# Gate and up of the feed-forward block: S1 T1 by a second Strassen level in four pairs, in one written order for three engines

## The chip, the cores and the metric

The kernel runs on one core of one Trainium2 chip. The metric is the device time of one execution in microseconds (us). All matrix products are done on TensorE (PE in the profile); VectorE (DVE) does the additions and subtractions, ScalarE (ACT) copies, the high parts and the GELU; SyncE (SP) and GpSimd (POOL) issue transfers between SBUF and DRAM.

## The reference, cut to what matters

```
x = A_x                                    # 1 x 2048 x 640
g = sigmoid((x * gate_w).sum(-1))
a = Re(DFT_seq(DFT_hidden(x)))             # DFT matrices given, as products
b = (gelu(x @ w_gate) * (x @ w_up)) @ w_down   # 640 -> 1728 -> 640
out = g * a + (1 - g) * b
```

All inputs are float32. The stage that the change touches is the pair of products `x @ w_gate` and `x @ w_up`.

## The kernel before, in words

Each float32 operand is split into a high part, rounded to the fp32r format of TensorE, and a low part, the rest. A product is then three matmuls of 128x128 by 128x512 (`mm3`): high times high, high times low, low times high. `split` makes the parts: the high one on ScalarE (`high`), the low one on VectorE (`low`), which needs the high one.

The 1728 hidden columns are 13 blocks of 128 and a rest of 64. Block 0 and the rest are computed first, plainly. Blocks f = 1 to 12 use Strassen's scheme with seven products on a two-by-two matrix whose rows of blocks are gate and up and whose columns are halves of the 640 inputs (the fifth 128 rows are extra products, `g5`, `u5` and `D`). The tokens are handled as two halves tp of two 512-token tiles each. The weights' sums are called S1 to S4, the tokens' sums T1 to T4; the results collect in PSUM banks X and Z.

Blocks 1 and 2 run through `gate_up`. From block 3 on, two blocks make a pair p (p = 1 to 5): `pair_first` computes the gate's and the up's first products of both blocks and both token halves by a second Strassen level (J = 1 and 2: sums of weights from `pair_parts`, sums of tokens from `cross_sums`, which go to the DRAM tiles `xtd` and come back by `load_cross`). Then `chain` runs for each of the two blocks and both token halves the other products: S1 T1, S2 T2, S3 T3, S4 with its extra product, and A22 T4. In the old kernel S1 T1 of a pair takes eight mm3 (two blocks, two token halves, two input halves), and a pair 70 mm3.

What sets the order: TensorE, VectorE and ScalarE each work through their instructions in the order of the built program. A scheduler of the language makes that order from the dependencies, except inside `in_order(...)`, where each named engine keeps the order in which the code was written. In the old pairs only TensorE has a written order, and only in `pair_first`. `seed` copies a PSUM bank into a new bank on ScalarE, so that two sums can go on from one partial sum. `chain_parts(f)` makes the four weight sums S1 to S4 of a block (four VectorE operations of 256 elements and one of 128), and splits them: 1024 elements on each of the two engines. `extras` puts other work into the pairs: weight sums for later stages (`sum_wd`, `sum_wu`, stored to DRAM) and the gate's row sums (`load_z`, a VectorE reduction). All loads are issued in order on SP's queue, most into a ring of 48 buffers (`slot`), where a new tile waits until the last use of its buffer is over; results are stored from POOL's queue (`keep`).

After the pairs comes the down stage (`load_k`, `split_k`, `step_k`), then the sequence DFT (the C stage: `load_c`, `split_c`), then the hidden DFT. From the down stage on, ScalarE and VectorE have a written order.

Of the kernel before, what the change touches and what calls it, by code (L numbers as in the profile page):

```python
# [23 lines left out]
NK = (NF - 1) // 2  # L24
XN_AT = [5, 10, 15, 20]
EORD = [0, 2, 1, 3, 4]


@with_exitstack
def kernel(  # L30
# [84 lines left out]
    uA, uT = ([[dram.tile([P, 4, T], F32, tag=f"u{n}{j}{p}", name=f"u{n}{j}{p}") for p in range(ND)] for j in range(2)] for n in "AT")  # L115
    xtd = {J: dram.tile([P, 3, 2, T], F32, tag=f"xtd{J}", name=f"xtd{J}") for J in (1, 2)}
    grd, gmd = (dram.tile([1, S], F32, tag=n, name=n) for n in ("grd", "gmd"))
# [22 lines left out]
    def load_x(tp):  # L140
# [23 lines left out]
        def tsum(i):  # L164

            a, b = {1: ((1, 2), (1, 1)), 2: ((2, 2), "T1"), 3: ((2, 2), (1, 2)), 4: ((2, 1), "T2")}[i]
            r[f"T{i}"] = pair(F32, f"xs{n}{i}")
            tt(r[f"T{i}"], r[a], r[b], op=ALU.subtract)
            B[f"T{i}"] = hl(f"xT{n}{i}")

        def his(*keys):
# [59 lines left out]

    def chain_parts(f, raw, W):

        ra, rb = raw
        sm, *c = wchunk(f"ws{f}")
        g01, g23, u23 = ra[:, 0:2], ra[:, 2:4], ra[:, 5:7]
        tt(sm[:, 0:2], rb, u23, op=ALU.add)
        tt(sm[:, 4:6], g01, rb, op=ALU.subtract)
        tt(sm[:, 2:4], sm[:, 0:2], g01, op=ALU.subtract)
        tt(sm[:, 6:8], g23, sm[:, 2:4], op=ALU.subtract)  # L240
        d = wsmall(F32R, f"wd{f}")
        split(*c, sm)
        tt(rb[:, 1], ra[:, 4], ra[:, 7], op=ALU.subtract)
        split(d[:, 0], d[:, 1], rb[:, 1])
        W["D"] = d[:, 0], d[:, 1]
        for i in range(2):
            for k in range(4):
                W[f"S{k + 1}", i] = at(c, 2 * k + i)

# [8 lines left out]
    def pair_parts(p, r0, r1):  # L258
# [16 lines left out]
        return W  # L275

    def cross_loads(J):

        r = [pair(F32, f"xc{J}{q}") for q in range(2)]
        for q in range(2):  # L280
            nc.sync.dma_start(r[q], xt[2 * q, 2 * J - 2 : 2 * J].rearrange("d p c -> p d c"))
        return r
# [138 lines left out]
    def pair_first(p, WP, W):  # L421
# [59 lines left out]
        return X, s1  # L481

    def chain(f, W, B, tp, s5, X, s1):

# [22 lines left out]
        tt(s2, s2, Z, op=ALU.add)  # L507
        last_products(X, W, B, tp, k, second, s1, s2, s5, prod)
        yield

    def last_products(X, W, B, tp, k, second, s1, s2, s5, prod):

# [3 lines left out]
        if second:  # L516
# [4 lines left out]
            keep(hT[tp][k], 1, t1)  # L521
        prod(X, "A22", "T4", False)
        mm3(X, W["u5"], at(B[5], 0), False, True)
        tt(s1, s1, X, op=ALU.mult)
        keep(hA[tp][k], 2 * second, s1)
        if second:
            tt(s5, s1, t1, op=ALU.subtract)
# [16 lines left out]
    def sum_wd(k):  # L544

        r, a21 = slot(F32, [P, 8, P], f"dr{k}"), wsmall(F32, f"da{k}")
        nc.sync.dma_start(r, wd[k, :, :8])
        nc.sync.dma_start(a21, wd[k, :, 8:])
        sums_left(f"d{k}", r, a21, wsd[k])

    def sum_wu(p):


        r, a21 = slot(F32, [P, 8, P], f"ur{p}"), wsmall(F32, f"ua{p}")
        nc.sync.dma_start(r, wu[p, :, :8])
        nc.sync.dma_start(a21, wu[p, :, 8:])
        if p > 1:
            v, r = r, slot(F32, [P, 8, P], f"un{p}")
            for a, b in ((0, 2), (2, 4), (4, 5), (5, 8)):
                kept = p == 4 and a in (0, 4)  # L560
                nc.scalar.activation(r[:, a:b], v[:, a:b], AF.Copy, scale=1.0 if kept else -1.0)
            if p < 4:
                v, a21 = a21, wsmall(F32, f"ub{p}")
                nc.scalar.activation(a21, v, AF.Copy, scale=-1.0)
            nc.gpsimd.dma_start(wneg[p], r)
        sums_left(f"u{p}", r, a21, wsu[p])

# [17 lines left out]
    def load_z(sb):  # L585

        r = slot(F32, [P, D], f"xz{sb}")
        nc.sync.dma_start(r, xz[sb])
        nc.vector.tensor_tensor_reduce(r, r, gwb, 1.0, 0.0, ALU.mult, ALU.add, z[:, sb : sb + 1])

# [312 lines left out]
    sq = [lambda k=k: sum_wd(k) for k in range(NK)]  # L903
    for p in range(ND):
        sq.insert(2 * p + 1, lambda p=p: sum_wu(p))

    def extras():
        sq.pop(0)()
        for _ in range(2):
            if zq:  # L910
                load_z(zq.pop(0))

# [25 lines left out]
    for i in (1, 2):  # L938
        for J in (2, 1):
            load_cross(J, i)  # L940
    chain_parts(3, raws[0], Ws[0])
    for p in range(1, NK):
        f = 2 * p + 1
        for J in (2, 1):
            load_cross(J, 4)
        with in_order(PE):
            X, s1 = pair_first(p, WP, Ws)
        for i in range(2):
            s5 = pair(F32, f"s5{f + i}")
            work = [chain(f + i, Ws[i], Bs[tp], tp, s5[:, tp], X[i, tp], s1[i, tp]) for tp in range(2)]  # L950
            for step in range(4):
                for w in work:
                    next(w)
                if (i, step) == (0, 0):
                    chain_parts(f + 1, raws[1], Ws[1])
                if i == 0 and step in (1, 3):
                    extras()
                if p == NK - 1:
                    if (i, step) == (0, 0):
                        gate_rows()  # L960
                    if (i, step) == (0, 2):
                        extras()
                    if (i, step) == (0, 3):
                        load_k(0)
                    if (i, step) == (1, 0):
                        split_k(0)
                    if i == 1 and step >= 1:
                        load_k(step)
                    continue
                if (i, step) == (0, 2):  # L970
                    nraws = load_raw(f + 2), load_raw(f + 3)
                if (i, step) == (1, 0):
                    raws = nraws
                    WP = pair_parts(p + 1, raws[0][0], raws[1][0])
                if (i, step) == (1, 1):
                    nWs = [plain_parts(f + 2 + i, raws[i][0]) for i in range(2)]
                    for J in (2, 1):
                        load_cross(J, 1)
                if (i, step) == (1, 2):
                    chain_parts(f + 2, raws[0], nWs[0])  # L980
                    load_cross(2, 2)
                if (i, step) == (1, 3):
                    load_cross(1, 2)
                    Ws = nWs
    order = ctx.enter_context(ExitStack())
# [360 lines left out]
```

## Time and profile before

| | us |
|---|---|
| median of three runs (lowest to highest) | 1026.31 (1026.24 to 1027.57) |
| the profiled execution | 1026.11 |
| its span | 1024.3 |
| TensorE busy, 4500 matmuls | 1017.2 |
| VectorE busy | 794.1 |
| ScalarE busy | 478.1 |

The span is what the trace covers; the execution's own time is a little longer. TensorE's busy time counts overlapping matmuls once, so an engine shown busy may still have some idle time between its matmuls; the spacing of matmuls in the timeline is the sharper measure. Of the span, the pairs p = 1 to 5 take the stretch from about 96 to 336 us.

### The profile page before, as it was taken

Reading aid. Unit: us, or ns where it says so; the run is one execution under the profiler, and the core shown is the slowest. Engines: PE = TensorE matmul, PEld = TensorE weight load, DVE = VectorE, ACT = ScalarE, POOL = GpSimd, SP = SyncE. Lnnn points to the kernel's source line nnn. Section 1 sums busy time; section 2 is a strip of 40 time slices with the busy share of each in tenths; the row PEclk is TensorE's granted clock in tenths of the full one; section 3 lists DMA queues with packets and bytes.
Section 4 is the critical chain, followed back from the end, with each engine's and each line's share of the span. In section 5 each row is a group of like instructions: output and inputs, shape, how many; then the busy total and the mean of one; then the engine's idle time right before and its main releaser. Section 6 shows DMA issues by size and latency. Waiting matters only on the chain.

```text
span 1024.3 us, 12988 instructions
## 1 busy us (share of the span) xinstructions
PE 1017.2 (99%) x4500; PEld 839.3 (82%) x4500; DVE 794.1 (78%) x1099; ACT 478.1 (47%) x631; POOL 137.4 (13%) x245
## 2 busy tenths in 40 slices
PE   9999999999999999999999999999999999999998
PEld 6888778888888888888888888888888888888887
DVE  6998777777866949976898966786577769697784
ACT  5455443555463647466355443444343354355430
POOL 0023121212122200100010011002000200021013
PEclk9999999999999999999999999999999999999999
DMA  8258767776888987867866677557666777897748
GB/s 300 80 205 278 273 246 269 256 273 240 301 286 328 389 319 251 272 245 267 310 202 232 214 223 263 191 195 243 240 203 209 276 258 287 290 331 219 269 97 131
DMA packets 84914, 255.04 MB, mean 249 GB/s; under 512 B 10768, under 2 KB 18992, under 8 KB 84848
## 3 DMA queue, kind: packets, MB, share of 16 engines
q1 hardware_dynamic: 63376, 187.13, 53.4%
q0 software_dynamic: 21328, 66.88, 19.3%
q8 instruction: 35, 0.57, 0.2%
q14 instruction: 31, 0.25, 0.1%
q10 hardware_dynamic: 144, 0.20, 0.1%
HBM read 187.04 MB, written 67.13 MB: 248 GB/s over the span
## 4 chain that ended last, share of the span: by engine, by line
PE 97%; DMA 2%; DVE 0%; ACT 0%; issue 0%; SPq 0%
PE pZ L87 5%; PE pZ L85 4%; PE pZ L86 4%; PE pX L85 4%; PE pX L87 4%; PE pX L86 4%; PE pL L85 3%; PE pL L86 3%; PE pL L87 3%; PE px L85 3%; PE px L86 3%; PE px L87 3%; PE pV L85 2%; PE pV L86 2%; PE pV L87 2%; DMA xx<-xtd 1%
## 5 line engine op out<-in xcount | busy, mean ns | idle before, releaser
L74 ACT ACTIVATE ch<-csa 128x1024 fp32r<-128x1024 f32 x32 | 34.0, 1062 | 88.4 <-DVE csa L638 53.8
L74 ACT ACTIVATE ch<-cra 128x1024 fp32r<-128x1024 f32 x32 | 33.9, 1058 | 48.5 <-DVE cl L77 18.1
L77 DVE TENSOR_TENSOR cl<-cra,ch 128x1024 fp32r<-128x1024 f32 x32 | 39.1, 1223 | 16.2 <-ACT ch L74 15.9
L77 DVE TENSOR_TENSOR cl<-crb,ch 128x1024 fp32r<-128x1024 f32 x32 | 39.1, 1222 | 15.0 <-ACT ch L74 8.3
L86 PE MATMUL pL<-cl,xah 128*128 128x512 f32 x128 | 49.8, 389 | 0.0
L87 PE MATMUL pL<-ch,xal 128*128 128x512 f32 x128 | 49.8, 389 | 0.0
L85 PE MATMUL pL<-ch,xah 128*128 128x512 f32 x128 | 49.3, 389 | 0.0
L77 DVE TENSOR_TENSOR cl<-csb,ch 128x1024 fp32r<-128x1024 f32 x32 | 39.2, 1224 | 6.2 <-ACT ch L74 4.7
L74 ACT ACTIVATE ch<-crb 128x1024 fp32r<-128x1024 f32 x32 | 33.8, 1055 | 19.5 <-DVE cl L77 7.8
L77 DVE TENSOR_TENSOR cl<-csa,ch 128x1024 fp32r<-128x1024 f32 x32 | 39.1, 1222 | 4.0 <-ACT ch L74 3.3
L307 POOL DMA_DIRECT2D hA<-s x48 | 26.1, 543 | 101.3 <-DVE s L514 39.8
L74 ACT ACTIVATE ch<-csb 128x1024 fp32r<-128x1024 f32 x32 | 33.9, 1059 | 11.9 <-PE pL L86 6.9
L513 ACT ACTIVATE s<-s 128x512 f32<-128x512 f32 x20 | 12.6, 630 | 56.2 <-DVE s L507 56.2
L77 DVE TENSOR_TENSOR kl<-kw,kh 128x1024 fp32r<-128x1024 f32 (+1 forms) x26 | 31.5, 1211 | 6.9 <-ACT kh L74 6.9
L74 ACT ACTIVATE kh<-kw 128x1024 fp32r<-128x1024 f32 (+1 forms) x26 | 27.1, 1041 | 10.8 <-DVE kw L696 3.5
L1052 POOL DMA_DIRECT2D uA<-s x16 | 8.7, 543 | 158.4 <-DVE s L1098 151.8
L307 POOL DMA_DIRECT2D hT<-s x48 | 26.1, 544 | 22.5 <-DMA hT<-s 5.1
L751 POOL DMA_DIRECT2D out<-ks x12 | 6.5, 543 | 167.3 <-DVE ks L750 166.7
L87 PEld LDWEIGHTS pL<-ch,xal 128*128 128x128 f32 x128 | 24.0, 188 | 5.0
L85 PEld LDWEIGHTS pL<-ch,xah 128*128 128x128 f32 x128 | 24.0, 188 | 5.0
L86 PEld LDWEIGHTS pL<-cl,xah 128*128 128x128 f32 x128 | 24.0, 188 | 5.0
L637 DVE TENSOR_TENSOR csa<-cra 128x512 f32<-128x512 f32 x32 | 22.0, 687 | 7.5 <-PE pL L86 6.5
(3041 smaller groups left out, 3407.4 us busy)
## 6 DMA issues: line engine op xcount, KB each, us to landing
cra<-in_ct SPq DMA_DIRECT2D x64, 512.0 KB, 4.0
crb<-in_ct SPq DMA_DIRECT2D x64, 512.0 KB, 4.8
xx<-xtd SPq DMA_DIRECT2D x30, 512.0 KB, 5.5
hA<-s POOLq DMA_DIRECT2D x48, 256.0 KB, 5.8
hT<-s POOLq DMA_DIRECT2D x48, 256.0 KB, 7.3
kr<-hA SPq DMA_DIRECT2D x24, 512.0 KB, 7.1
kr<-hT SPq DMA_DIRECT2D x24, 512.0 KB, 7.1
ux<-uA SPq DMA_DIRECT2D x24, 512.0 KB, 5.2
```

What stands on the lines that cost most here:

```text
L74: nc.scalar.activation(hi, raw, AF.Copy)
L77: nc.vector.tensor_tensor(lo, raw, hi.bitcast(F32), op=ALU.subtract)
L85: nc.tensor.matmul(ps, lh, rh, start=first, stop=False, skip_group_check=True)
L86: nc.tensor.matmul(ps, lh, rl, start=False, stop=False, skip_group_check=True)
L87: nc.tensor.matmul(ps, ll, rh, start=False, stop=last, skip_group_check=True)
L307: nc.gpsimd.dma_start(to[:, i], src)
L513: nc.scalar.activation(s2, s2, AF.Gelu_apprx_tanh)
L637: tt(s1[:, 0], r1[:, 1], r1[:, 0], op=ALU.subtract)
L751: nc.gpsimd.dma_start(out[2 * tp + t, e], src)
L1052: nc.gpsimd.dma_start(to[:, i], src)
```

## The change

Pairs 2 to 5 no longer run `pair_first` and `chain` but one generator, `whole_pair`. Pair 1 stays as it was, and gains the sums for a third token set, J = 3, made of T1 (which is kept in DRAM, `xt1`). In a whole pair S1 T1 of both blocks and both token halves is done by seven mm3 with the second level's sums (`fifth_parts`, banks `Z`), so a pair has 69 mm3. Its `yield` numbers count mm3; what else has to be done is written between them, in `in_order(PE, ACT, DVE)`. Three of the weight sums (`sum_wu` for p = 2 to 4) move from the pairs into the C stage, at its steps 17, 20 and 34, and are computed one step after their loads are issued. `chain_parts`, `sum_wd`, `sum_wu` and `load_z` now return their arithmetic as a function, to be called later. The weights' parts of block f (`chain_parts(f)`), which were made in the pair before, are now made inside the pair.

```diff
+WU_AT = [17, 20, 34]
...
-    def chain_parts(f, raw, W):
+    def chain_parts(f, raw, W, again=False):
...
+        tt(rb[:, 1], ra[:, 4], ra[:, 7], op=ALU.subtract)
         d = wsmall(F32R, f"wd{f}")
-        split(*c, sm)
-        tt(rb[:, 1], ra[:, 4], ra[:, 7], op=ALU.subtract)
-        split(d[:, 0], d[:, 1], rb[:, 1])
...
+        def parts():
+            split(*c, sm)
+            split(d[:, 0], d[:, 1], rb[:, 1])
+            if again:
+                W["raw"] = mtile(F32, f"wr{f}")[:, : 2 * P].rearrange("q (i c) -> q i c", i=2)
+                nc.scalar.activation(W["raw"], sm[:, 0:2], AF.Copy)
...
+    def fifth_parts(p, W0, W1):
+
+        a, b = W0["raw"], W1["raw"]
+        e = mtile(F32, f"fs{p}").rearrange("q (k c) -> q k c", k=4)
+        tt(e[:, 0], b[:, 0], b[:, 1], op=ALU.add)
+        tt(e[:, 2], a[:, 0], b[:, 0], op=ALU.subtract)
+        tt(e[:, 1], e[:, 0], a[:, 0], op=ALU.subtract)
+        tt(e[:, 3], a[:, 1], e[:, 1], op=ALU.subtract)
+        h = slot(F32R, [P, 2, 4, P], f"fh{p}")
+        split(h[:, 0], h[:, 1], e)
...
+    def whole_pair(p, WP, Ws, raws):
...
+        yield 3
+        m(v00, 2, "a12", "b21")
+        m(va, 2, "s2", "t2")
+        v01 = seed(va, f"pv01{p}")
+        m(X[0, 0], 1, "a12", "b21")
+        m(xa_, 1, "s2", "t2")
+        X[0, 1] = seed(xa_, f"px01{p}")
+        sv, sx = copy(ve, f"sv{p}"), copy(xe, f"sx{p}")
+        s1[0, 0] = copy(X[0, 0], f"s100{p}")
+        yield 7
+        fifth(v00, 0, "g5", 0, 0)
+        plus(s1[0, 0], v00)
+        m(v01, 2, "s4", "b22")
+        m(va, 2, "s3", "t3")
+        v10 = seed(va, f"pv10{p}")
+        yield 10
...
+        prod(X[0, 0], 0, "S2", "T2", 0)
+        state(0, 0)
+        plus(s1[1, 1], sv)
+        yield 19
...
+        fifth(Z[0, 1], 0, "u5", 1, 1)
+        plus(Z[0, 1], sz)
+        nc.scalar.activation(s5[0][:, 1], Z[0, 1], AF.Copy)
+        plus(s5[0][:, 1], X[0, 1])
+        m(Z[1, 0], 3, "a22", "t4")
+        yield 38
...
+        with in_order(PE, ACT, DVE):
+            for u in whole_pair(p, WP, Ws, raws):
+                if u == 3:
+                    parts = chain_parts(f, raws[0], Ws[0], True)
+                    for i in (1, 2, 4):
+                        load_cross(3, i)
+                if u == 7:
+                    parts()
+                if u == 13:
+                    parts = chain_parts(f + 1, raws[1], Ws[1])
+                if u == 16:
+                    parts()
+                if u == 19:
+                    WP[3] = fifth_parts(p, *Ws)
+                    todo = extras()
+                if u == 29:
+                    if todo:
+                        todo.pop(0)()
+                    todo += extras()
+                if u == 38:
+                    for do in todo:
+                        do()
+                if more:
+                    if u == 32:
+                        nraws = load_raw(f + 2), load_raw(f + 3)
+                    if u == 47:
+                        nWP = pair_parts(p + 1, nraws[0][0], nraws[1][0])
...
+                else:
+                    if u == 47:
+                        gate_rows()
+                        load_k(0)
...
+                    if u == 59:
+                        split_k(0)
...
+        if i in WU_AT:
+            wu_sums = sum_wu(2 + WU_AT.index(i))
+        if i - 1 in WU_AT:
+            wu_sums()
```

**Place 1, the end of pair 2 on ScalarE in the old program.** `ws7h` is the high part of the sums of block 7, the first of pair 3; `vh3`, `ve3` are parts of the second-level weights of pair 3; `pva3` and `pxa3` are the first banks of pair 3; `pZ6` is bank Z of block 6.

```order
L497 ACTIVATE s56_1628<-pZ6_0_1629 128x512
L497 ACTIVATE s56_1628<-pZ6_1_1640 128x512
L132 ACTIVATE s26_0_1672<-px102_1440 128x512
L74 ACTIVATE vh3_1652<-vs3_1651 128x1024
L132 ACTIVATE s26_1_1680<-pxa2_1377 128x512
L74 ACTIVATE ve3_1654<-wa7_1552 128x512
L74 ACTIVATE wp7_1682<-wa7_1552 128x512
L74 ACTIVATE wp8_1685<-wa8_1556 128x512
L74 ACTIVATE wd7_1713<-wb7_1553 128x128
L74 ACTIVATE ws7h_1707<-ws7r_1706 128x1024
L513 ACTIVATE s26_0_1672<-s26_0_1672 128x512
L513 ACTIVATE s26_1_1680<-s26_1_1680 128x512
```

In the old program the first seed of pair 3 is the row behind these, so `ws7h` stands ahead of all its seeds; and the copies of Z6 stand ahead of `vh3`.

The same `ws7h` on ScalarE in the changed program, inside pair 3. `px013`, `pv103` and `px103` are seeds into new banks, `sv3`, `sx3`, `s1003` and `s1013` copies from banks.

```order
L444 ACTIVATE px013_1873<-pxa3_1825 128x512
L134 ACTIVATE sv3_1875<-pve3_1826 128x512
L134 ACTIVATE sx3_1877<-pxe3_1827 128x512
L134 ACTIVATE s1003_1879<-px003_1836 128x512
L75 ACTIVATE ws7h_1845<-ws7r_1844 128x1024
L75 ACTIVATE wd7_1852<-wb7_1612 128x128
L254 ACTIVATE wr7_1885<-ws7r_1844 128x256
L444 ACTIVATE pv103_1897<-pva3_1824 128x512
L534 ACTIVATE s1003_1879<-s1003_1879 128x512
L134 ACTIVATE s1013_1904<-px013_1873 128x512
L444 ACTIVATE px103_1909<-pxa3_1825 128x512
```

It has moved between the seeds: ahead of `pv103` and `px103`, which TensorE's steps 14 and 16 use, and behind the seed and copies that step 7 feeds.

**Place 2, VectorE at the same place of the changed program**, up to the second block's sums `ws8r`.

```order
L78 TENSOR_TENSOR ws7l_1846<-ws7r_1844,ws7h_1845 128x1024
L78 TENSOR_TENSOR wd7_1852<-wb7_1612,wd7_1852 128x128
L531 TENSOR_TENSOR s1003_1879<-s1003_1879,pv003_1831 128x512
L531 TENSOR_TENSOR px013_1873<-px013_1873,sx3_1877 128x512
L531 TENSOR_TENSOR pxa3_1825<-pxa3_1825,sx3_1877 128x512
L531 TENSOR_TENSOR s1013_1904<-s1013_1904,pv013_1865 128x512
L241 TENSOR_TENSOR ws8r_1918<-wb8_1616,wa8_1615 128x256
L242 TENSOR_TENSOR ws8r_1918<-wa8_1615,wb8_1616 128x256
L243 TENSOR_TENSOR ws8r_1918<-ws8r_1918,wa8_1615 128x256
L244 TENSOR_TENSOR ws8r_1918<-wa8_1615,ws8r_1918 128x256
L245 TENSOR_TENSOR wb8_1616<-wa8_1615 128x128
L531 TENSOR_TENSOR s1013_1904<-s1013_1904,sv3_1875 128x512
```

The low part `ws7l` stands ahead of the additions to `s1003` and `px013`, and the sums of block 8 ahead of the last addition to `s1013`. In the old program these additions follow one another, with `ws7l` ahead of the pair and the `ws8r` sums behind all of them.

**Place 3, ScalarE near the end of pair 3 in the changed program.** `s27` are the gated values of block 7, `vh4`, `ve4`, `vq4` parts of pair 4's second-level weights, `pz103` and `pza3` the banks Z of block 8.

```order
L685 ACTIVATE s27_0_1955<-s27_0_1955 128x512
L685 ACTIVATE s27_1_1980<-s27_1_1980 128x512
L75 ACTIVATE vh4_2127<-vs4_2126 128x1024
L75 ACTIVATE ve4_2129<-wa9_2043 128x512
L75 ACTIVATE vq4_2130<-wa10_2047 128x256
L634 ACTIVATE s58_1823<-pz103_2057 128x512
L634 ACTIVATE s58_1823<-pza3_1989 128x512
```

The copies of the second block's Z, which stood ahead of the next pair's `vh`, now stand behind `vh4`, `ve4` and `vq4`, and these behind two GELUs whose input VectorE makes after the gate reductions.

More of the change, by code (lines that the diff above doesn't have):

```diff
@@ L588, in load_z @@
         nc.sync.dma_start(r, xz[sb])
[L589 removed]
+        return lambda: nc.vector.tensor_tensor_reduce(r, r, gwb, 1.0, 0.0, ALU.mult, ALU.add, z[:, sb : sb + 1])
     xa, xb = {}, {}
@@ L940 @@
             load_cross(J, i)
-    chain_parts(3, raws[0], Ws[0])
-    for p in range(1, NK):
+    chain_parts(3, raws[0], Ws[0])()
+    p, f = 1, 3
+    for J in (2, 1):
+        load_cross(J, 4)
+    with in_order(PE):
+        X, s1 = pair_first(p, WP, Ws)
+    for i in range(2):
+        s5 = pair(F32, f"s5{f + i}")
+        work = [chain(f + i, Ws[i], Bs[tp], tp, s5[:, tp], X[i, tp], s1[i, tp]) for tp in range(2)]
+        for step in range(4):
+            for w in work:
+                next(w)
+            if (i, step) == (0, 0):
+                chain_parts(f + 1, raws[1], Ws[1])()
+            if (i, step) == (0, 1):
+                xc[3] = cross_loads(3)
+            if (i, step) == (0, 3):
+                t3[3] = cross_sums(3, xc[3])
+            if (i, step) == (1, 1):
+                split(Bs[1]["T1"][0][:, 0], Bs[1]["T1"][1][:, 0], t3[3])
+            if i == 0 and step in (1, 3):
+                for do in extras():
+                    do()
+            if (i, step) == (0, 2):
+                nraws = load_raw(f + 2), load_raw(f + 3)
+            if (i, step) == (1, 0):
+                raws = nraws
+                WP = pair_parts(2, raws[0][0], raws[1][0])
+            if (i, step) == (1, 1):
+                Ws = [plain_parts(f + 2 + i, raws[i][0]) for i in range(2)]
+                for J in (2, 1):
+                    load_cross(J, 1)
+            if (i, step) == (1, 2):
+                load_cross(2, 2)
+            if (i, step) == (1, 3):
+                load_cross(1, 2)
@@ L972 @@
[L972 to L984, printed above, removed]
+                        load_k(2)
@@ L985 @@
+                    if u == 65:
+                        load_k(3)
+        if more:
+            raws, WP, Ws = nraws, nWP, nWs
     order = ctx.enter_context(ExitStack())
```

210 lines of the change are left out of this document (160 added, 50 removed).

## The prediction

> **What bounds the kernel now.** I read the page first, then who waits for whom on TensorE, then the busy times of the pair stage by stretch, then the timelines of single engines in pair 3. A "pair" is two of the blocks f; pairs 2 to 5 are the four that change.
>
> ```profile
> span 1024.3 us, 12988 instructions
> ...
> PE 1017.2 (99%) x4500; PEld 839.3 (82%) x4500; DVE 794.1 (78%) x1099; ACT 478.1 (47%) x631; POOL 137.4 (13%) x245
> ...
> PE 97%; DMA 2%; DVE 0%; ACT 0%; issue 0%; SPq 0%
> ```
>
> The chain that ended last is TensorE's matmuls for 97% of the span. The profiled execution took 1026.11 us, 1.8 more than its span and 0.2 under the median of the three runs, 1026.31.
>
> ```profile
> PE px L85 <- DMA xx<-xtd: 0.6, 1, 0.6
> PE pxa L85 <- DMA xx<-xtd: 0.6, 1, 0.6
> ```
>
> These are TensorE's only waits behind the first 10 us (us in total, times, longest). So every matmul taken away is worth its full spacing, and every wait put in front of a matmul costs its full length.
>
> ```profile
> L85 PE MATMUL pva<-x021h,ve x1: 389/389/389, 144.3 to 144.3; 128*128 128x512 f32 x1
> 205.37 0.39 PE L85 MATMUL pZ<-xT01h,ws7h 128*128 128x512 f32 x1
> ...
> 240.73 0.39 PE L85 MATMUL pva<-x021h,ve 128*128 128x512 f32 x1
> ...
> 336.25 0.39 PE L85 MATMUL kX<-kb0000h,kh 128*128 128x512 f32 x1
> ```
>
> From 205.37 to 240.73 stand 156 matmuls without a gap: 0.2267 us each, so one mm3 (three matmuls, called a step below) takes 0.68. Pairs 2 to 5 run from 144.3 to 336.25, that is 191.95 us; their 840 matmuls need 190.4, so they hold 1.5 us of small gaps.
>
> ```profile
> core 0: us, PE busy (x) PEld busy (x) DVE busy (x) ACT busy (x) POOL busy (x), PEclk, DMA share, GB/s
> 95.78:143.60 47.82, 47.19 (x208) 38.71 (x207) 38.32 (x77) 22.20 (x38) 9.47 (x18) 1.00 0.71 245
> 192.57:240.73 48.16, 48.16 (x213) 39.51 (x212) 37.76 (x73) 23.12 (x42) 10.84 (x20) 1.00 0.75 271
> 600.00:700.00 100.00, 100.00 (x443) 82.81 (x442) 71.69 (x85) 39.04 (x43) 9.79 (x18) 1.00 0.66 221
> ```
>
> In a pair VectorE is busy 38 of 48 us and ScalarE 23. Neither is full, so the question is not how much work they get, but **what stands ahead of the results that TensorE asks for**, now that each of them must follow the written order.
>
> **Durations used.** VectorE, then ScalarE, each row a start and a length:
>
> ```profile
> 201.03 0.39 PE L87 MATMUL px<-x111h,vl 128*128 128x512 f32 x1
> 201.46 0.70 DVE L465 TENSOR_TENSOR px<-px,sx 128x512 f32<-128x512 f32 x1 [1.31 <-PE px L87]
> 203.41 0.68 DVE L439 TENSOR_TENSOR s<-s,pv 128x512 f32<-128x512 f32 x1
> 204.13 0.69 DVE L439 TENSOR_TENSOR s<-s,sv 128x512 f32<-128x512 f32 x1
> 207.43 0.42 DVE L237 TENSOR_TENSOR ws8r<-wb,wa 128x256 f32<-128x256 f32 x1
> 207.76 0.42 DVE L238 TENSOR_TENSOR ws8r<-wa,wb 128x256 f32<-128x256 f32 x1
> 208.44 0.29 DVE L243 TENSOR_TENSOR wb<-wa 128x128 f32<-128x128 f32 x1
> 208.64 0.42 DVE L240 TENSOR_TENSOR ws8r<-wa,ws8r 128x256 f32<-128x256 f32 x1
> 211.23 1.23 DVE L77 TENSOR_TENSOR ws8l<-ws8r,ws8h 128x1024 fp32r<-128x1024 f32 x1 [1.84 <-ACT ws8h L74]
> 218.53 0.82 DVE L589 CUSTOM_DVE_ANT_0 xz<-xz,gwb 128x640 f32<-128x640 f32 x1
> ...
> 219.28 0.69 DVE L514 TENSOR_TENSOR s<-s,s 128x512 f32<-128x512 f32 x1
> 219.88 0.68 DVE L524 TENSOR_TENSOR s<-s,px 128x512 f32<-128x512 f32 x1
> 229.01 1.22 DVE L77 TENSOR_TENSOR vl<-vs,vh 128x1024 fp32r<-128x1024 f32 x1
> 230.14 0.68 DVE L77 TENSOR_TENSOR ve<-wa,ve 128x512 fp32r<-128x512 f32 x1
> ```
>
> ```profile
> 202.19 0.58 ACT L418 ACTIVATE px<-pxa 128x512 f32<-128x512 f32 x1 [0.78 <-PE pxa L87]
> 202.69 0.59 ACT L132 ACTIVATE s<-px 128x512 f32<-128x512 f32 x1
> 204.85 0.63 ACT L440 ACTIVATE s<-s 128x512 f32<-128x512 f32 x1 [0.71 <-DVE s L439]
> 205.39 0.58 ACT L132 ACTIVATE s<-px 128x512 f32<-128x512 f32 x1
> 210.14 1.05 ACT L74 ACTIVATE ws8h<-ws8r 128x1024 fp32r<-128x1024 f32 x1
> 211.09 0.59 ACT L132 ACTIVATE s<-px 128x512 f32<-128x512 f32 x1
> 235.08 1.06 ACT L74 ACTIVATE ws9h<-ws9r 128x1024 fp32r<-128x1024 f32 x1
> ```
>
> From start to start, on VectorE: 0.60 for 512 elements, 0.72 where it needs the one before, 0.34 for 256, 0.20 for 128, 1.13 for 1024, 0.75 for a gate reduction. On ScalarE: 0.50 for a copy from PSUM, 0.54 for a gelu, 0.95 for 1024. A hand-over between them takes 0.04 us (204.13+0.69 to 204.85), and a step's result is usable 0.43 after its last matmul starts (201.03 to 201.46). Note the last row: the 1024-element weight split ws9h runs at 235, well ahead of pair 4's start at 240.73, with TensorE on other work.
>
> **What goes.** Gate and up lose one step a pair (69 for 70): 12 matmuls, 12 x 0.2267 = **-2.7 us**. The 1.5 us of gaps in the old pairs go too, since I count the new ones anew.
>
> **What the written order adds.** I set t=0 at step 0's third matmul (its first two now stand ahead of the previous pair's step 57). Step n then starts at 0.68n-0.45, and its result is there at 0.68n+0.43. I walk the lists of ScalarE and VectorE in their order.
>
> A. Step 7 ends at 5.19. ScalarE then does px01, sv, sx and s100 (to 7.15), the split ws7h (to 8.20), wd7 and wr7, and only then the seed pv10: done at 9.3, wanted at 9.1 by step 14. VectorE's ws7l waits for ws7h (8.24), and behind it stand s100 and px01 (10.2 to 10.9). ScalarE's copy s101 waits for that, and the seed px10 stands behind the copy: done at 12.0. Step 16 wanted it at 10.4. TensorE is late by **1.6**.
>
> B. From 12.0 VectorE adds to pxa and s101, makes the five sums of ws8 (13.2 to 14.9), and adds sv (15.6). ScalarE's gelu waits for that, then ws8h (to 17.2), wd8, and the copy s27_0 (17.9). Step 22 must not add to its bank before that copy; late already, it would come at 16.1. **+1.9**.
>
> C. VectorE takes ws8l at 17.25, wd8l, two adds (to 20.0), and the four fs sums one after the other (20.9); ScalarE's fh high part ends at 21.6, VectorE's low part at 22.35. The third matmul of step 25 would come at 20.5. **+1.9**, so 5.4 so far.
>
> D. With that lag step 37 ends at 31.0; an add, a copy and an add leave VectorE free at 33.0. Now come four gate reductions and a weight sum (4 x 0.75 + 1.4), two gated blocks with a gelu each in between (to 41.5), one up block (42.8) and the four sums of the next pair's vs (44.3). ScalarE's vh, ve, vq and the copy of Z10 follow: ve at 45.9, the copy at 46.8. The next pair's first two matmuls want ve at 43.7 and step 57 wants the copy. **+2.7**. A pair thus takes 69 x 0.68 + 8.1 = 55.0, and VectorE ends its list 5.7 us into the next pair, just in time not to make A worse.
>
> E. In pairs 3 and 4 the buffer of ws7h (ws9h) was the s5 pair whose last store goes out when VectorE has written it, 2.4 us into the pair.
>
> ```profile
> DMA to landing us min/median/max: 2.7/7.2/11.7
> ```
>
> These are the stores to hT. At the median ws7h may be written at 9.7 instead of 7.15: **+2.5** in these two pairs; bounds 0 and 7.
>
> F. Pair 5 has A to C (5.4), no reductions and no vs, but gate_rows in TensorE's order behind step 47:
>
> ```profile
> L570 ACT ACT_TABLE_LOAD x1 | 1.3, 1283 | 0.0
> ```
>
> The sigmoid stands behind two gelus (37.0) and a table load, so the transposition waits until 38.5 instead of 37.6: +1.0. Then the first three 1024-element lows of the down stage stand on VectorE ahead of the up blocks whose banks that stage wants; by the same count +1.3.
>
> Sum: 8.1 + 10.6 + 10.6 + 7.7 = 37.0 us of waits, less 2.7, less 1.5: **+32.8**, and 1026.11 + 32.8 = 1058.9.
>
> Costed at nothing: the three more cross loads a pair (issued behind steps 3, 5 and 6, wanted at step 25, nine us later; were one late, its whole lateness would count). The sums of xtd3 in pair 1: VectorE there gets 2.4 + 1.13 + 1.2 us and loses some 2.9 of ws5, at 38.3 busy of 47.8; between -1.2 (the two waits above) and +2. The three weight sums in the C stage: 1.4 us of VectorE and some 2 of ScalarE each, at 72 and 39 us busy of 100, two steps ahead of their use; 0 to 4 if that cover were gone. The transfers of T1 to DRAM at the start: 0 to 1.
>
> **A rule weighed.** The granted clock is 1.00 in each row above, and the longest idle time of TensorE in this trace is the first:
>
> ```profile
> 1.20 3.06 PE L858 MATMUL pwarm<-warm 128*128 128x512 bf16 x7 [1.20 <-DVE warm L815]
> ```
>
> Those seven are spaced (3.06-0.61)/6 = 0.41 us, 0.18 more than later ones; so a cold start costs 7 x 0.18 = 1.3 us here. My longest new idle time is some 2.8 us (step 14 in pairs 3 and 4).
> The Trainium skill, "TensorE: Matmul & The Clock Gate", "The HAM clock gate", has the clock fall to half after an idle window of about 3.4 us; by it no wait of this forecast is long enough, and the sum stays, but one grown by another us would be. No trace here shows such a fall in mid-run.
>
> **The rivals.**
> 1. *It does what it says, and the two engines keep up.* Then only -2.7, and 0 to -1.5 of the old gaps: 1022 to 1023.4. For it: no engine is full. Against it: even without any wait, ScalarE's list between step 7's end and px10 is 5.6 us long, and step 16 comes 5.2 after it. It holds if ws7h's 0.95 could pass the seeds, which a written order rules out.
> 2. *Only A costs*, the rest being absorbed, since TensorE's own lateness gives the others time: 4 x 1.6 - 4.2 = +2.2, 1028.3; with half of B to D, 1040.
> 3. *The clock falls* at waits of 2 to 3 us: one to two cold starts a pair, 4 x 1.3 to 8 x 1.3 = 5 to 10 more: 1064 to 1069.
> 4. *Nothing to be seen*: waits of 1 us a pair eat the 2.7 to 4.2 that is gained, 1024 to 1028. It needs ScalarE's list alone to decide.
>
> **How the numbers follow.** Forecast (1045 to 1064): 0.68. Rival 1: 0.05. Rival 2 up to 1045: 0.12. Rival 3: 0.10. Rival 4: 0.05. About 0.2% (2 us) is what a measurement of this kernel can tell from no change. Slower by more: 0.68+0.12+0.10 = 0.90; within: 0.05; faster: 0.05. Forecast, rival 3 and the upper end of rival 2 lie within 1038 to 1069; the bounds of E (0 to 7, twice) are the widest of the unknowns and lie mostly within it too. Time: 1059.
>
> **What would show it.** In the changed profile pairs 2 to 4 should be 55 to 58 us long, with TensorE waiting at px10 for ScalarE, at the first S3 T3 product for the copy s2, at fh, and at ve or the copy of Z; C-stage and down-stage stretches should be as long as before. I am wrong if a pair is under 49 us; if the waits name DMA instead, SP's queue has become the bound; if E is off, pairs 2 and 3 are equally long. A granted clock under 1.00 in a pair would speak for rival 3.

## The result, and the profile after

The changed kernel takes 1060.27 us (median of 4 runs, 1059.33 to 1063.66) against 1026.51 for the kernel before on the same chip: a ratio of 1.0333, with a 95% interval of 1.0308 to 1.0357. It is slower. The profiled execution took 1060.79 us, with a span of 1059.0, 34.7 more than before.

The head of the page of the changed kernel, and its chain that ended last by engine:

```profile
span 1059.0 us, 13091 instructions
...
PE 1026.5 (97%) x4488; PEld 838.2 (79%) x4488; DVE 811.6 (77%) x1134; ACT 489.1 (46%) x658; POOL 141.1 (13%) x251
...
PE 73%; issue 16%; POOL 4%; DVE 3%; DMA 2%; ACT 1%; POOLq 0%; DVEq 0%; ACTq 0%
```

Twelve matmuls fewer are there (4488 for 4500), and the chain is no longer TensorE alone. What TensorE waits for behind the first 10 us (us in total, times, longest):

```profile
PE px L86 <- ACT s L134: 8.9, 4, 4.4
PE pva L86 <- ACT ve L75: 6.1, 3, 2.1
PE px L86 <- ACT px L444: 4.5, 4, 1.1
PE pze L86 <- ACT fh L75: 4.0, 3, 1.4
...
PE pv L86 <- ACT pv L444: 1.0, 2, 0.6
PE pgr L750 <- issue: 1.0, 1, 1.0
```

Before there were two such waits of 0.6. Now each of the four pairs waits at a seed (px or pv) and at the copy s2 (s); three wait at fh (in pair 2 the longer wait at s2 stands for it), and three times ve is waited for, at the end of pairs 2 to 4. In order of time, TensorE's rows of the waits in pairs 2 and 4 (the wait in brackets), with the third matmul of step 0 of pairs 2 to 5 and the first of the down stage:

```profile
143.71 0.39 PE L88 MATMUL pva<-x021h,ve 128*128 128x512 f32 x1
...
164.48 0.50 PE L86 MATMUL px<-xT03h,ws5h 128*128 128x512 f32 x1 [4.36 <-ACT s L134]
...
192.54 0.80 PE L86 MATMUL pva<-x021h,ve 128*128 128x512 f32 x1 [2.04 <-ACT ve L75]
...
202.87 0.39 PE L88 MATMUL pva<-x021h,ve 128*128 128x512 f32 x1
...
249.50 0.50 PE L86 MATMUL pva<-x021h,ve 128*128 128x512 f32 x1 [2.05 <-ACT ve L75]
...
260.19 0.39 PE L88 MATMUL pva<-x021h,ve 128*128 128x512 f32 x1
...
269.79 0.50 PE L86 MATMUL pv<-xx,vq 128*128 128x512 f32 x1 [0.37 <-ACT pv L444]
272.59 0.50 PE L86 MATMUL px<-xx,vq 128*128 128x512 f32 x1 [1.15 <-ACT px L444]
278.46 0.50 PE L86 MATMUL px<-xT03h,ws9h 128*128 128x512 f32 x1 [1.50 <-ACT s L134]
282.16 0.50 PE L86 MATMUL pze<-xx,fh 128*128 128x512 f32 x1 [1.36 <-ACT fh L75]
306.55 0.50 PE L86 MATMUL pva<-x021h,ve 128*128 128x512 f32 x1 [2.04 <-ACT ve L75]
...
315.64 0.39 PE L88 MATMUL pva<-x021h,ve 128*128 128x512 f32 x1
...
368.87 0.61 PE L86 MATMUL kX<-kb0000h,kh 128*128 128x512 f32 x2
```

Pair 4 is the plain one: 55.45 us, that is 69 x 0.68 = 46.9 and 8.5 of waits with their restarts. (Each wait costs more than its bracket: the matmul behind it starts 0.34 later instead of 0.23.) The four pairs are 59.16, 57.32, 55.45 and 53.23 us, together 37.5 over 4 x 46.9. By busy time and granted clock (the column of 1.00s, behind POOL's), the four pairs are:

```profile
143.71:202.87 59.16, 51.55 (x208) 40.36 (x207) 41.20 (x81) 24.46 (x44) 10.83 (x20) 0.94 0.73 258
202.87:260.19 57.32, 50.59 (x209) 39.47 (x207) 40.66 (x79) 24.05 (x43) 9.93 (x19) 0.97 0.69 243
260.19:315.64 55.45, 48.97 (x208) 38.30 (x207) 39.06 (x77) 23.30 (x42) 9.64 (x18) 1.00 0.72 254
315.64:368.87 53.23, 48.29 (x207) 38.05 (x206) 32.84 (x57) 27.05 (x46) 9.74 (x18) 1.00 0.77 270
```

VectorE works 39 to 41 us of 55 to 59 in the first three: it is not full, it is late. And the clock is under 1.00 in pairs 2 and 3: it halved three times, behind the waits at 164.48, 192.54 and 249.50, for some 3.4 us each (counted in slices of 1 us). The same wait at 306.55 brought no fall: from there to the next pair took 9.09 us, from 249.50 on 10.69. So that fall seems to cost 1.6 us, and the one at 192.54 (10.33 us to 202.87) 1.24.

Pair 2 has a wait of its own, of 4.36 instead of 1.50. One row of VectorE shows where it begins, with the sums of ws6 written into a buffer that a store to hT still reads:

```profile
159.78 0.42 DVE L241 TENSOR_TENSOR ws6r<-wb,wa 128x256 f32<-128x256 f32 x1 [2.77 <-DMA hT<-s]
```

Outside the pairs the time hardly moved: pair 1 ends 1.05 us earlier, the down stage up to the C stage takes 1.4 more, and the C stage 1.0 more in this execution.

### The profile page after: what moved, and what is told of

Its sections match the earlier page's. It is cut to its first block, busy times and chain, and to the rows that moved or that the text cites. A ratio compares the mean times of both kernels' runs of the same rounds, so it can differ in the third digit from the quotient of the medians.

```text
span 1059.0 us, 13091 instructions
## 1 busy us (share of the span) xinstructions
PE 1026.5 (97%) x4488; PEld 838.2 (79%) x4488; DVE 811.6 (77%) x1134; ACT 489.1 (46%) x658; POOL 141.1 (13%) x251
## 4 chain that ended last, share of the span: by engine, by line
PE 73%; issue 16%; POOL 4%; DVE 3%; DMA 2%; ACT 1%; POOLq 0%; DVEq 0%; ACTq 0%
PE pX L86 3%; PE pX L88 3%; PE pX L87 3%; PE pL L88 3%; PE pL L87 3%; PE pL L86 3%; POOL hT L333 2%; POOL hA L333 2%; PE pZ L88 2%; PE pZ L87 2%; PE pZ L86 2%; PE pV L88 2%; PE pV L86 1%; PE pV L87 1%; DMA hA<-s 1%
## 5 line engine op out<-in xcount | busy, mean ns | idle before, releaser
L685 ACT ACTIVATE s<-s 128x512 f32<-128x512 f32 x20 | 12.6, 631 | 60.4 <-DVE s L531 50.8
L1275 POOL DMA_DIRECT2D uA<-c x8 | 4.4, 544 | 169.8 <-DVE c L1362 169.6
```

Source lines behind the costliest of these rows:

```text
L685: nc.scalar.activation(s2, s2, AF.Gelu_apprx_tanh)
L1275: nc.gpsimd.dma_start(to[:, i], src)
```

## The experiments

**Which engine's order.** Three kernels drop the written order of one or both of the other engines in the four pairs; the scheduler then orders those, as before the change.

```diff
-        with in_order(PE, ACT, DVE):
+        with in_order(PE):          # e1_pe_only
+        with in_order(PE, DVE):     # e2_act_free
+        with in_order(PE, ACT):     # e3_dve_free
             for u in whole_pair(p, WP, Ws, raws):
```

> The four pairs keep TensorE's written order; ScalarE and VectorE are ordered by the scheduler there, as they were before the change. Theory (the cost is the written order of the two engines: waits A to D, and the clock falls that those waits bring): most of A to D goes, no granted clock under 1.00 in a pair, pairs of 47 to 50 us, and 1022 to 1032 us in all. Rival 'second level' (the new products need their sums and seeds later than any order of the two engines can give them): the waits at px10, s2, fh and ve stay within a half of what they are, over 1045 us. Rival 'transfers' (buffers held by stores decide): the wait of VectorE for the store to hT stays, waits name DMA, over 1045 us.

> TensorE and VectorE in written order in the four pairs, ScalarE ordered by the scheduler. Theory: A (ScalarE's split ahead of the seeds) and most of B (the copy of s27 behind the gelu and the split) go, C and D (VectorE's lists) stay: about 4 x 3.5 = 14 us less than the changed kernel, 1042 to 1050 us. If the written order of VectorE alone makes all the waits: 1057 to 1061. If ScalarE's alone: as with both free, under 1035.

> TensorE and ScalarE in written order in the four pairs, VectorE ordered by the scheduler. Theory: D goes (reductions and sums need not stand ahead of the next pair's vs) and the clock falls behind it, C shrinks, A and B stay: 3 x 2.1 + 2.8 of falls + about 4 of C less than the changed kernel, 1044 to 1052 us. If ScalarE's written order makes all the waits: 1057 to 1061. If VectorE's alone: under 1035.

Measured: e1 1034.18 us (ratio to the kernel before 1.0087, 1.0070 to 1.0104), e2 1058.31 (1.0327, 1.0303 to 1.0352), e3 1041.94 (1.0159, 1.0145 to 1.0173). TensorE's waits in e1:

```profile
PE px L86 <- ACT s L134: 3.3, 1, 3.3
PE pze L86 <- ACT fh L75: 2.7, 4, 2.2
```

and in e2:

```profile
PE pze L86 <- ACT fh L75: 15.1, 4, 6.9
PE pva L86 <- ACT ve L75: 7.1, 3, 3.0
PE px L86 <- ACT s L134: 1.6, 3, 1.1
```

The 26 us that e1 gains are what the two orders cost together, the falls of the clock that they bring included; the new products themselves can be fed in time. e1 lies over its theory's 1022 to 1032, since the clock still fell in pair 2. In its sum e2 did not follow the theory. With ScalarE free the waits at the seeds and most of those at s2 are gone, as expected, but 15.1 + 1.6 us at fh and s2 stand against the 18.4 of A to C in the changed kernel.

Pair by pair it looks different. Pair 5 is undisturbed up to fh: neither VectorE nor ScalarE waits for a transfer, and the clock stays at 1.00. TensorE's row at fh in it, in the changed kernel, e2, e3 and e1:

```profile
337.25 0.50 PE L86 MATMUL pze<-xx,fh 128*128 128x512 f32 x1 [1.33 <-ACT fh L75]
336.07 0.50 PE L86 MATMUL pze<-xx,fh 128*128 128x512 f32 x1 [1.72 <-ACT fh L75]
318.26 0.50 PE L86 MATMUL pze<-xx,fh 128*128 128x512 f32 x1 [0.22 <-ACT fh L75]
312.69 0.50 PE L86 MATMUL pze<-xx,fh 128*128 128x512 f32 x1 [0.21 <-ACT fh L75]
```

The pair's start, the third matmul of step 0, is at 315.64, 316.22, 300.00 and 295.77 us. So from the start to fh it takes 21.61 us with both orders written, 19.85 with VectorE's alone, 18.26 with ScalarE's alone and 16.92 with neither. Of the 4.7 us that A to C cost there, VectorE's order alone makes 2.9 and ScalarE's alone 1.3. Each of the two has its part, VectorE's more than twice as large. e2 gains in pair 3 as well (19.3 us up to fh, 22.2 in the changed kernel), but not in pairs 2 and 4 (24.3 for 24.5, and 21.5 for 22.0). There VectorE waits for a buffer that a store to hT holds, 2.8 us at ws6r and 3.05 at ws9l, TensorE then waits 6.86 and 3.93 us at fh, and by the granted clock it runs at half speed for 6.8 us in each of the two:

```profile
268.34 1.23 DVE L78 TENSOR_TENSOR ws9l<-ws9r,ws9h 128x1024 fp32r<-128x1024 f32 x1 [3.05 <-DMA hT<-s]
```

D is VectorE's alone: the wait for ve stays in e2 (7.1 us) and is gone in e3.

What is left in e1 stands in pair 2, 56.7 us long against 47.4 to 47.6 for the others.

**The three weight sums alone.**

```diff
 # the kernel before
-    for p in range(ND):
-        sq.insert(2 * p + 1, lambda p=p: sum_wu(p))
+    for p in range(2):
+        sq.insert(2 * p + 1, lambda p=p: sum_wu(p)())
...
+        if i in WU_AT:
+            wu_sums = sum_wu(2 + WU_AT.index(i))
+        if i - 1 in WU_AT:
+            wu_sums()
```

> The kernel before, with nothing but the last three weight sums of the up gradients moved to the C stage. Theory (the C stage of the changed kernel is 1.0 us longer because a split there waits for the buffer that the store of the negated weights holds): C stage 0.7 to 1.0 us longer than before, the pairs 0 to 0.5 shorter, 1026.5 to 1027.5 us. Rival (the sums move the time in the pairs, where VectorE loses work): 1023 to 1025.5 us. Rival (they are free): 1026.3 within 0.3.

1025.69 us, ratio 1.0001 (0.9992 to 1.0010): free. The split there does wait 4.0 us for the store of the negated weights, and TensorE does not notice. From its first product to the first of the up gradients the C stage takes 391.7 us in the kernel before, 392.7 in the changed one, and 391.6 to 392.2 in all twelve experiments, which have the sums at the same place. The 1.0 us of the changed kernel is one wait of TensorE for a copy of ScalarE, at 692.99 us, of 0.68 us and with its restart of 0.95; the stage has no other. ScalarE's split 13 us ahead of it had waited 5.90 us for the store of the negated weights, the longest of these thirteen traces (4.0 to 5.5 in the others). e5, with 5.4, is the only other one with a listed wait at that place, of 0.24 us. So these sums are free while that store lands early enough; that its late landing makes the 1.0 us is likely, but no run shows it by itself.

**The buffer in pair 2.** Moving three loads changes which buffers the next tiles get.

```diff
 # e1 (e5), the changed kernel (e11)
                 if u == 3:
                     parts = chain_parts(f, raws[0], Ws[0], True)
-                    for i in (1, 2, 4):
-                        load_cross(3, i)
+                    if p > 2:
+                        for i in (1, 2, 4):
+                            load_cross(3, i)
...
                     parts = chain_parts(f + 1, raws[1], Ws[1])
+                    if p == 2:
+                        for i in (1, 2, 4):
+                            load_cross(3, i)
                 if u == 16:
```

> As e1 (TensorE alone in written order in the four pairs), and in the first of them the three cross loads of xtd3 stand behind the sums of the second block's weights instead of ahead of them, so that ws6r gets a buffer which no store holds. In e1 that pair was 56.7 us long and the next three 47.4 to 47.6. Theory (the excess is one wait for a buffer held by a store to hT, and the clock falls it brings): that pair becomes 47 to 49 us, no granted clock under 1.00, 1023 to 1026 us in all, so 0 to 0.25% faster than the kernel before. Rival (the transfers themselves are too many there and whatever waits for them comes as late: the loads now come late at step 25): the pair stays over 52 us and the total over 1029.

> The changed kernel, all three engines in written order, with the cross loads of xtd3 moved as in e5 in the first of the four pairs alone. Theory (the 4.4 us wait there is the 1.5 of the other pairs and 2.8 for a buffer that a store to hT holds): that pair is 2.8 to 4 us shorter, the other pairs as they were, 1056 to 1058 us. Rival (the two engines' lists take it back): 1059.5 to 1061.

e5 took 1027.68 us (1.0019, 1.0009 to 1.0029), more than the theory's 1023 to 1026; pair 2 fell from 56.7 to 50.8 us, and no clock fell. Most of the excess was that one buffer, but not all of it. In e11 (1059.74 us; 1.0332, 1.0318 to 1.0347) the same edit gave next to nothing: its pair 2 is 2.3 us shorter, with the 4.36 down to 1.51 and a new wait of 1.37 at fh, and pair 3, behind whose wait for ve at its end no clock fell, 2.1 shorter, but pair 4 is 3.0 longer. ScalarE's row there says why:

```profile
266.47 1.06 ACT L75 ACTIVATE ws9h<-ws9r 128x1024 fp32r<-128x1024 f32 x1 [3.20 <-DMA hT<-s]
```

This is term E: the split waits for a buffer that a store holds. In the changed kernel it waited 0.25 there. It comes back when TensorE reaches the pair earlier, here because the fall behind step 57 is missing. In pair 3 of e11, which has the fall in front of it, ws7h does not wait for a store at all. The next runs show it again.

**The clock.** Six matmuls into a bank that the next product overwrites fill most of the wait in front of step 57.

```diff
                     plus(s5[1][:, tp], X[1, tp])
+                if p < NK - 1:
+                    for _ in range(2):
+                        mm3(X[0, 0], WP[3]["a11"], b[3]["b11"], True, True)
                 yield 56
```

> The changed kernel with six more matmuls (1.36 us, into a bank that the next product overwrites) in front of step 57 of the first three pairs, so that TensorE idles 0.7 us there instead of 2.04. Theory (the falls of the granted clock at 192 and 250 us come of that idle time): no granted clock under 1.00 behind step 57, the two falls' 1.2 and 1.6 us gone: 1057 to 1058.3 us. Rival (the falls come of something else, or the restart costs the same): 1060 to 1061.

The wait for ve was 0.7 us in all three pairs and the clock stayed at 1.00 behind it, so those falls did come of the idle time. But the kernel took 1063.09 us (1.0368, 1.0354 to 1.0382), more and not less. ScalarE's rows:

```profile
213.25 1.06 ACT L75 ACTIVATE ws7h<-ws7r 128x1024 fp32r<-128x1024 f32 x1 [2.70 <-DMA hT<-s]
...
270.57 1.06 ACT L75 ACTIVATE ws9h<-ws9r 128x1024 fp32r<-128x1024 f32 x1 [2.08 <-DMA hT<-s]
```

In the changed kernel the two waits are 0.52 and 0.25. VectorE's list, which writes what the store takes, runs on through a fall (from vl to the first sum of ws7 or ws9 it takes 15.1 us in both kernels); so the 1.2 to 1.6 us that a fall takes from TensorE are time in which the store lands. Without the fall ScalarE comes to the split that much earlier and waits that much longer. The other 0.9 us in pair 3 and 0.2 in pair 4 are a store that landed later. TensorE waits behind it, 2.82 us at pv instead of 0.64, and 2.20 instead of 0.37. And behind these two longer waits the clock falls instead:

```profile
216.00:218.00 2.00, 2.00 (x5) 1.07 (x4) 0.97 (x2) 1.61 (x3) 0.00 (x0) 0.50 0.71 247
274.00:276.00 2.00, 1.34 (x3) 0.58 (x3) 0.85 (x2) 1.41 (x3) 0.00 (x0) 0.50 0.67 241
```

So e8 moved two falls and did not remove them: counted in slices of 1 us, TensorE ran at half speed for 17 us of its pairs and for 10 us in the changed kernel. The moved ones cost nothing that can be seen. From pv to fh both pairs take 12.38 us, and 12.37 in the changed kernel without a fall there, because the waits between shrank by as much. Nor was anything gained at step 57: from ve to fh it takes 33.5 and 32.9 us, with the falls there 32.6 and 32.7. Half of the 2.8 us that e8 is slower was lost in pair 2 ahead of the edit's first place (4.90 us at s2 and a fall of 6.8 us), so it can't be put down to the six matmuls.

**Moving A or D within the written order.**

```diff
 # e7_a_late
-                if u == 7:
+                if u == 13:
                     parts()
 # e6_d_late
-                if u == 38:
+                if u == (62 if more else 38):
                     for do in todo:
                         do()
```

> The changed kernel, all three engines in written order; the split of the first block's weight sums (ws7h, ws7l, wd, wr) stands behind the seeds pv10 and px10 instead of ahead of them (term A), in all four pairs. Theory 'each wait for itself': A goes, 4 x 2.0 us, B and C stay: 1051 to 1053 us. Rival 'one list' (VectorE and ScalarE owe the same work by step 25, so that the lateness is only taken at another place): waits at px10 go, waits at s2 and fh grow by as much, 1057 to 1062 us.

> The changed kernel, all three engines in written order; the gate reductions and the down-weight sum that stood ahead of the next pair's vs (term D) stand behind both gated blocks and up blocks now (in the first three of the four pairs). Theory 'each wait for itself': D goes in three pairs, 3 x 2.6, and the clock falls behind it, 1.2 + 1.6: 1049 to 1051 us. Rival 'one list' (VectorE's list is as long as before, so what is not waited for at the end of a pair is waited for in the next one's A to C): A to C grow by what D loses, 1056 to 1061 us, the falls apart.

e7: 1060.77 us (1.0344, 1.0329 to 1.0360), no change. The waits at px10 are gone, and those at the copy s2 grew to 2.20 in pairs 3 and 4 (1.50 before the edit), with 0.5 for ws7l or ws9l in front; from the pair's start to fh both take 21.8 us, in the changed kernel 22.2 and 22.0. "One list" holds: as long as both orders are written, moving the split within them only moves the wait.

e6: 1078.46 us (1.0509, 1.0493 to 1.0525), a miss for both theories. The wait for ve is gone, and this stands in its place:

```profile
PE pva L86 <- DMA xx<-xtd: 12.3, 3, 4.2
...
PE pxe L86 <- DMA xx<-xtd: 5.2, 2, 2.8
```

The next pair's cross loads take the buffers of the gate rows that the reductions free (already in the changed kernel SP's queue waits three times there for a reduction, 19.9 us in all, without TensorE waiting for it). With the reductions behind the up blocks the first of these loads went out at 194.3 us, in the changed kernel at 184.1. The lump stood early for a reason that neither theory had.

**D at another place.** The reductions earlier instead of later, in VectorE's idle time:

```diff
-                    todo = extras()
+                    todo = extras() + extras()
                 if u == 29:
-                    if todo:
-                        todo.pop(0)()
-                    todo += extras()
-                if u == 38:
-                    for do in todo:
+                    for do in todo[:3]:
+                        do()
+                if u in (32, 36, 38):
+                    for do in todo[{32: 3, 36: 4, 38: 5}[u] :][: 1 if u < 38 else None]:
                         do()
```

> The changed kernel, all three engines in written order; the gate reductions and weight sums of a pair, which stood in one lump of 4.4 us behind step 36 (term D), stand behind fh, at steps 32, 36 and 38 now, where VectorE idles (6.5 us in all between fh and the lump); their loads go out 10 steps earlier. Theory (VectorE's list is the bound and its idle time there is free): D goes in three pairs, 3 x 2.6, A to C unchanged: 1051 to 1054 us. Rival (D's lateness is taken at another place): 1057 us or more. If the loads' buffers collide, waits name DMA.

1052.66 us (1.0263, 1.0249 to 1.0277), in the range of the theory. The wait for ve is gone in all three pairs (3 x 2.65 with its restarts: from fh to the next pair, pair 4 takes 30.83 us, in the changed kernel 33.48), and so are the two falls behind it (2.8 us); but ws7h and ws9h wait 1.50 and 2.15 for the store now, 2.9 more than in the changed kernel:

```profile
207.48 1.06 ACT L75 ACTIVATE ws7h<-ws7r 128x1024 fp32r<-128x1024 f32 x1 [1.50 <-DMA hT<-s]
262.17 1.06 ACT L75 ACTIVATE ws9h<-ws9r 128x1024 fp32r<-128x1024 f32 x1 [2.15 <-DMA hT<-s]
```

-8.0 - 2.8 + 2.9 = -7.9, measured -7.6 between the medians. D was a cost of its own; E is what was hidden behind it.

**TensorE's steps.** The product that needs fh stands two steps later, the first S3 T3 product one step later.

```diff
+        m(za, 3, "a11", "b11", True)
+        Z[0, 0] = seed(za, f"pz00{p}")
         prod(X[0, 0], 0, "S3", "T3", 0)
         yield 23
-        m(za, 3, "a11", "b11", True)
-        Z[0, 0] = seed(za, f"pz00{p}")
-        m(ze, 3, "s1", "t1", True)
-        sz = copy(ze, f"sz{p}")
         gelu(s1[1, 1])
         prod(X[0, 1], 0, "S3", "T3", 1)
+        m(ze, 3, "s1", "t1", True)
+        sz = copy(ze, f"sz{p}")
```

> As e5, and in TensorE's order of the four pairs the third pair product of Z (the one that needs fh) stands two steps later and the first S3 T3 product (which needs the copy s2) one step later. In e5 TensorE lost 0.70 us at fh in each of the last three pairs and 0.96 at each of the two places in the first. Theory (these two results come 0.5 to 1 us late for the order of e5, and nothing else is late): 3 x 0.7 + 1.9 = 4.0 us less than e5, 1023 to 1025 us, 0.1 to 0.3% faster than the kernel before. Rival (the two engines are late as a whole, so the wait only moves on): 1026.5 to 1028.

> The three edits of e9, e10 and e11 together, all three engines in written order. Theory 'each wait for itself': 1060.3 less 3 for the buffer, 7.9 for D, and 4 x 2.6 for the steps moved at s2 and fh: 1038 to 1041 us. Rival 'one list' (moving TensorE's steps frees nothing in the lists of the two other engines; only the lump does): 1048 to 1052 us.

e12, the three edits in written order: 1053.91 us (1.0286, 1.0259 to 1.0312), no better than e10 alone and 1.9 us over the range of its rival "one list"; its trace has three falls in the pairs, that of e10 one. The wait at fh is gone, and 2.5 us at the next product that needs a copy of ScalarE's stand in its place, once in each pair:

```profile
PE px L86 <- ACT s L134: 12.8, 8, 2.5
```

Again one list: giving TensorE something else to do first does not make VectorE and ScalarE earlier while both keep the written order.

e9, the same edit on top of e5: **1023.30 us, ratio 0.9977 (0.9969 to 0.9986)**, faster than both kernels. Its head, its waits behind the first 10 us, and the four pairs by busy time and clock:

```profile
span 1020.1 us, 13083 instructions
```

```profile
PE px L86 <- ACT s L134: 0.2, 1, 0.2
PE px L86 <- DMA xx<-xtd: 0.2, 1, 0.2
```

```profile
143.75:191.75 48.00, 47.80 (x208) 38.55 (x207) 41.02 (x83) 25.02 (x44) 11.38 (x22) 1.00 0.89 311
191.75:238.87 47.12, 47.12 (x208) 38.71 (x207) 40.24 (x81) 24.12 (x43) 10.85 (x21) 1.00 0.88 305
238.87:285.79 46.92, 46.92 (x208) 38.86 (x207) 39.02 (x79) 27.22 (x46) 9.79 (x19) 1.00 0.87 304
285.79:332.41 46.62, 46.62 (x207) 38.50 (x206) 30.86 (x55) 25.95 (x44) 8.04 (x16) 1.00 0.83 301
```

The pairs are at 69 x 0.68 = 46.9 us, with as much VectorE work as in the changed kernel. Here the results were only late by half a microsecond to one, at two places, and moving the two places was enough.

## Why the prediction came out

The time was forecast at 1059 and came out at 1060.27, and the sign and the reason hold: what stands ahead of TensorE's operands in the lists of the two other engines costs more than the twelve matmuls give. By its steps:

- **What goes** (-2.7 and -1.5): right within a microsecond, as e9 shows, where the waits are gone: its four pairs take 188.7 us, and 191.95 - 4.2 would be 187.75.
- **A to D**: the sum was 8.1 a pair, pair 4 has 8.5, and the places are the ones named: px10, the copy s2, fh, ve. With their restarts A to D take about 2.1, 1.8, 1.9 and 2.65 us there, where 1.6, 1.9, 1.9 and 2.7 were forecast. The prediction walked both lists through in time, so its sum is that of one chain, and it was right. What would be wrong is to read A, B and C as three costs that can be taken away one by one: e7 and e12 each take one of these waits away and find it at the next place. Only D was apart (e10). Nor does what stands just ahead of a wait say whose order makes it: of the 4.7 us up to fh in pair 5, VectorE's order alone makes 2.9 and ScalarE's alone 1.3 (e2 against e3).
- **E** (2.5 in pairs 3 and 4): the mechanism was right, and in the changed kernel it is nearly unseen, 0.52 and 0.25 us. It had been worked out as if TensorE ran at full clock. With the clock halved behind step 57 the pair starts later against VectorE's list, and the store has nearly landed when ScalarE reaches the split. Where the clock did not fall or D was gone, E was 1.5 to 3.2 us (e8, e10, e11).
- **The clock**: Rival 3 came true in its mechanism, three falls in pairs 2 and 3. In the prediction's working no wait was long enough; waits of 2.04 and 2.05 us were, besides the one of 4.36. The rule weighed there (the Trainium skill, "TensorE: Matmul & The Clock Gate", "The HAM clock gate": a fall after an idle window of about 3.4 us) does not agree with these rows, and the measurement decides. That the total still fits is partly luck: the falls at step 57 (2.8 us) stand where E (5 us forecast, 0.8 found) was counted, and pair 2, 4.1 us over its forecast, makes up for pair 4, 2.1 under.
- **Missed**: the buffer of ws6r in pair 2, 2.77 us and a fall behind it. The prediction looked for the holders of ws7h's and ws9h's buffers alone, not of every buffer that the moved sums take. With it pair 2 is 12.2 over its steps, where 8.1 was forecast, and its 59.16 us lie outside the 55 to 58 named for pairs 2 to 4. The remark that pairs 2 and 3 would be equally long if E were off could not decide anything for that reason.
- **F**: pair 5 was forecast at 46.9 + 6.4 = 53.3 and measured 53.23, with 0.98 for the gate rows (1.0 forecast) and 1.4 behind it in the down stage (1.3).
- **Costed at nothing**: the weight sums in the C stage are free in e4, and may cost up to 1.0 us where their store lands late, as in the profiled execution of the changed kernel. The transfers of T1 and the sums of xtd3 in pair 1 cost nothing that can be seen there: pair 1 ended 1.05 us earlier.

What stays open: whether it is that store that makes the 1.0 us in the C stage, which of VectorE's instructions carry its 2.9 us of A to C, and what makes pair 2 of e9 still 1 us longer than the rest (its two waits of 0.2 explain less than half).

## What to carry to other kernels

A written order on an engine that is 70% busy can cost more than the work it saves, as VectorE's did here. What paid here was to write down the order of the engine that sets the time, to leave the others to the scheduler, and to give TensorE's own steps one or two places of slack where a result is late; the same slack inside the written order gave nothing (e12). When waits follow one another in a list, take one away and look where the lateness goes before counting the rest as separate gains, and look at each stretch by itself: in its sum e2 hid what its undisturbed pairs show. An instruction that seems to stand too early or too late may be there for the buffer that it frees or takes, so look up who gets that buffer before moving it.

## What was not expected of the hardware

The granted clock halved here after much shorter idle times than the prediction allowed for, but not always. In the twelve traces of the changed kernel and the experiments that change its pairs, 11 of 11 waits of TensorE over 3.8 us in these stages were followed by a fall, 13 of 29 between 2.0 and 3.4 us that met it at full clock, and none under 1.8 us. Equal waits differ: 2.04 us at 192.54 and 306.55 of the changed kernel, one with and one without.

```profile
192.00:194.00 2.00, 1.46 (x4) 1.07 (x5) 2.00 (x3) 2.00 (x5) 0.00 (x0) 0.62 0.14 55
194.00:196.00 2.00, 2.00 (x6) 1.61 (x5) 1.97 (x4) 0.29 (x1) 0.65 (x2) 0.52 0.83 246
196.00:198.00 2.00, 2.00 (x10) 1.61 (x9) 1.88 (x4) 0.09 (x1) 0.43 (x1) 1.00 0.73 279
...
306.00:308.00 2.00, 1.39 (x5) 0.87 (x6) 1.99 (x3) 2.00 (x5) 0.00 (x0) 1.00 0.40 162
```

Matmuls are spaced 0.43 us in a fall instead of 0.23. By the granted clock in slices of 1 us most falls last 3.4 us, some 6.8 (in e2, e3, e7 and e8), and the one in e1 10.2. And a fall while TensorE does not set the pace costs nothing that can be seen: from pv to fh it took 12.38 us with one (e8) and 12.37 without (the changed kernel).
